# A linear-attention layer and an MLP on one core: a new order of work, w spread by TensorE, and other places for loads and transposes

## The chip, the cores and the metric

The kernel runs on one core of a Trainium2 chip. The core has TensorE (PE, with its weight loads as PEld), VectorE (DVE), ScalarE (ACT), GpSimd (POOL) and SyncE (SP), which here only issues DMAs. The time is the device time of one execution in microseconds; before the change the median of 5 runs is 155.71 us (155.5 to 156.21).

## The reference

There are 4 batches, 8 heads, 768 time steps and 48 elements per head. For each head a state of 48 by 48 is carried through time; then every row of 384 elements is normalized and goes through an MLP of width 1,536 with ReLU, and is added to itself.

```python
for t in range(S):
    kt, vt, rt = (k[:, :, t].copy(), v[:, :, t].copy(), r[:, :, t].copy())
    cur = np.einsum('bhd,bhe->bhde', u[None] * kt, vt)
    y[:, :, t] = np.einsum('bhd,bhde->bhe', rt, state + cur)
    state = w[None, :, :, None] * state + np.einsum('bhd,bhe->bhde', kt, vt)
...
mu = np.mean(x, axis=-1, keepdims=True)
var = np.mean((x - mu) ** 2, axis=-1, keepdims=True)
xn = (x - mu) / np.sqrt(var + 1e-06) * g_ln
ch = np.maximum(xn @ w_ch1, 0.0) @ w_ch2
return (x + ch).astype(np.float32)
```

## The kernel before

The 768 steps of each batch are cut into 6 chunks of 128, which makes 24 tiles of 128 rows. A tile's K, R and V are loaded by SP as 128 partitions by 8 heads of 48 (steps LK, LR, LV, lines 347, 350, 353): 1,024 pieces of 192 bytes each, into rings of 10 buffers.

The decay is put into factors: `Fr` is w to the power of the position and `Fk` w to the power of minus the position less one, both made once by ACT from ln(w) (FR, FK, lines 310 and 307). SR and SK multiply R and K by them. TR transposes both on PE into the PSUM tile `tr`, TC copies them out, AT makes the 128x128 scores of each head, and AM (DVE, line 413) keeps the causal half and writes bf16. S adds up the chunk's keys times values into the state, ZU and ZD scale the state by w to the power of 128; for the tiles in `ZPE` the old state is added on PE by a product with the identity (line 441) and no ZD is needed. Y sums the state's part and the scores' part. The term with u is a number `cc` for each row and head: either PE makes it from the product Q and u's columns (line 434, copied by CC), or, for the tiles in `CC_BY_DVE`, it comes from two products KU and KR and a sum on DVE (line 456). VB (POOL) is that number times V, and X (DVE) adds Y and VB and gives the row's sum.

XN subtracts the mean and gives bf16, SQ (ACT) sums squares, RS (POOL) makes the inverse deviation. The normalized rows are transposed, either by PE and a copy (LT, XT) or by a DMA transpose (LTD). `K_BY_DMA` lists the tiles whose K is transposed by DMA too (TKD, and TRD for R). `GROUPS` says how many tiles go through the first matmul of the MLP together, one or two. UP is one PSUM bank of that matmul (12 instructions of 128 columns for a single tile, 6 of 256 for a pair); its number is 16 times the group, plus which bank. RL is the ReLU. DN is a third of the second matmul of one tile: its number is 4 times the tile, plus the third. OT scales and adds the row, STO stores it.

w1 comes in three thirds of 1,536/3 columns: LW1 loads one as fp32 from SP (line 330), and three steps SW scale it by minus g_ln into bf16 (ACT, DVE or POOL); SW 0 to 2 belong to third 0, 3 to 5 to third 1, 6 to 8 to third 2. For a single tile bank m of UP needs third m. IW2 loads a third of w2 and turns it into bf16 on the way, issued by POOL (line 344). DN third d needs third d of w2 and bank d of the hidden rows.

WU and DU are dummy matmuls on a zero tile that keep PE busy in the head (the number is how many).

All the order is written by hand. `PLAN` is a list of steps "name,number,engine" (v is DVE, s ACT, g POOL); each is emitted in turn, and every engine takes its own instructions in that order, SP its loads, transposes and stores as well. Nothing is reordered later; waits between engines are put in by the framework.

```python
for step in PLAN.split():
    name, i, e = step.split(",")
    steps[name](int(i), e)
```

How w is taken is set by `W_ROWS`. With it WF (line 220) loads w into all 128 partitions, LN (line 268) takes the logarithm of all, and FR and FK read it from SBUF. Without it the row is one partition, and WBM (line 272) spreads its logarithm by an fp32 product with a column of ones into the PSUM tile `y`, which FR and FK read:

```python
RB = P if W_ROWS else 1
...
nc.tensor.matmul(out=t[:, :C], lhsT=ones[:], rhs=ln_b[:], start=True, stop=True)
...
return ln_b[:].rearrange("p (h d) -> p h d", h=H) if W_ROWS else psum["ln"]
```

u's row and g_ln's row are loaded by ACT's queue (RI) after LN; UR on POOL multiplies u by w, and CU on PE turns the rows into columns. The rows of u times w in all partitions, for KU, are made later by UWR from loads LUB (u) and, without `W_ROWS`, LWB (w, line 384).

Of the kernel before, what the change touches and what calls it, by code (L numbers as in the profile page):

```python
# [10 lines left out]
ACT = mybir.ActivationFunctionType  # L11
ENG = mybir.EngineType

GROUPS = [1, 1, 1, 1, 1, 1, 2, 2, 2, 2, 2, 2, 2, 2, 1, 1]
ZPE = [1, 2, 3]
K_BY_DMA = [16, 17, 18, 19, 20, 21, 22, 23]
CC_BY_DVE = [10, 11, 12, 13, 14, 15, 16, 17, 18, 19, 20, 21, 22, 23]
W_ROWS = True
SLOTS = {'kf': 10, 'rf': 10, 'vf': 10, 'sck': 3, 'scr': 3, 'vv': 4, 'trs': 3, 'q': 2, 'A': 2, 'cc': 4, 'ku': 2, 'kr': 2, 'Z': 3, 'ZS': 2, 'Vb': 3, 'x': 13, 'xn': 3, 'xT': 4, 'hT': 4, 'ot': 3}
PLAN = """  # L20
MW,0,v WF,0,- TL,0,s MI,0,g MP,0,v WU,13,- MM,0,g LK,0,- LN,0,s LR,0,- RI,0,s DU,10,-
CL,0,- FR,0,s LW1,2,- FK,0,s SR,0,v SK,0,v DU,12,- TR,0,- WL,0,s LR,1,- LV,0,- UR,0,g
LK,1,- TCk,0,s DU,18,- CU,0,- SR,1,g CV,0,s TCr,0,v LK,2,- SK,1,v AT,0,- LR,2,- UW,0,s
Q,0,v UGC,0,s TR,1,- SW,6,s SW,8,v LV,1,- SW,7,v S,0,- AMa,0,v CC,0,s LV,2,- TCk,1,s
SK,2,g AMb,0,v TCr,1,s LW1,0,- DU,16,- Y,0,- CV,1,s ZU,0,v CV,2,s SR,2,g DU,6,- AT,1,-
Q,1,v VB,0,g DU,5,- TR,2,- AMa,1,v S,1,- TC,2,s AMb,1,v IW2,0,g LW1,1,- IW2,1,g X,0,v
CC,1,s SW,1,s Q,2,v DU,13,- AT,2,- IW2,2,g XN,0,v Y,1,- SW,0,s AM,2,v SW,2,g LT,0,-
SQ,0,s LR,3,- XT,0,v VB,1,g ZU,1,v DU,15,- UP,2,- X,1,v S,2,- RL,2,s SW,3,v SW,5,v
XN,1,s DU,1,- UP,0,- CC,2,v SR,3,v SW,4,s VB,2,g LT,1,- LK,3,- DU,1,- Y,2,- RL,0,s
UP,1,- XT,1,s RS,0,g LV,3,- ZU,2,v UP,18,- SK,3,v SQ,1,s LR,4,- DN,0,- RL,1,s X,2,v  # L30
TR,3,- RS,1,g LK,4,- RL,18,s UP,16,- TC,3,v XN,2,s CV,3,v AT,3,- RL,16,s Q,3,v UP,17,-
SR,4,v SQ,2,s SK,4,g AM,3,v LT,2,- S,3,- RS,2,g LK,5,- XT,2,v Y,3,- TR,4,- CC,3,v
RL,17,s LV,4,- UP,32,- VB,3,g TC,4,s DN,1,- LR,5,- X,3,v RL,32,s UP,34,- Q,4,v XN,3,s
LK,6,- SK,5,v AT,4,- ZU,3,v RL,34,s LT,3,- UP,33,- AM,4,v XT,3,s SQ,3,s CV,4,g UP,50,-
RL,33,s SR,5,v RS,3,g S,4,- RL,50,s Y,4,- CC,4,v TR,5,- ZU,4,v LR,6,- VB,4,g UP,48,-
TC,5,s SK,6,v DN,2,- ZD,4,g LV,6,- X,4,v AT,5,- OT,0,v LV,5,- UP,49,- SQ,4,s Q,5,v
XN,4,s DN,4,- SR,6,v RS,4,g LK,7,- RL,49,s LT,4,- S,5,- DN,5,- XT,4,s CC,5,v LUB,0,-
CV,6,g AM,5,v TR,6,- CV,5,g LR,7,- DN,6,- RL,48,s VB,5,g LK,8,- Y,5,- SK,7,v TC,6,s
UP,64,- UWR,0,g X,5,v LV,12,- UP,66,- XN,5,s Q,6,v SR,7,g AT,6,- RL,64,s LV,7,- OT,1,v
LT,5,- SQ,5,s S,6,- DN,8,- XT,5,v SK,8,g LR,9,- CC,6,v AM,6,v RL,66,s TR,7,- RS,5,g  # L40
UP,81,- LR,8,- ZU,6,v UP,80,- VB,6,g TC,7,v LR,10,- DN,9,- RL,81,s SR,9,g Q,7,v LK,9,-
AT,7,- CV,7,s Y,6,- SR,8,g DN,10,- RL,80,s X,6,v LV,8,- UP,82,- OT,2,v SQ,6,s LK,10,-
S,7,- AM,7,v XN,6,s SR,10,g DN,12,- CC,7,s RL,82,s LR,12,- LT,6,- DN,13,- VB,7,g ZU,7,v
CV,8,s XT,6,v Y,7,- STO,0,- ZD,7,g TR,8,- LK,11,- X,7,v DN,14,- SK,10,g TC,8,v XN,7,s
UP,65,- LV,10,- Q,8,v SK,9,g LT,7,- AT,8,- RL,65,s LK,12,- XT,7,v S,8,- KU,10,v SQ,7,s
UP,96,- SK,11,g OT,3,v LV,9,- CC,8,s TR,9,- AM,8,v UP,101,- VB,8,g TC,9,s LR,11,- DN,16,-
ZU,8,v RS,6,g RL,96,s STO,1,- Y,8,- Q,9,v CV,9,s DN,17,- ZD,8,g LK,16,- X,8,v CV,12,s
S,9,- RL,101,s KR,10,v AT,9,- LK,14,- CC,9,s XN,8,s SK,12,v TR,10,- VB,9,g SQ,8,s AM,9,v
UP,99,- LR,20,- TC,10,s DN,18,- SR,11,g ZU,9,v LV,11,- UP,97,- CV,10,s CC,10,v ZD,9,g RL,99,s
AT,10,- OT,4,v STO,2,- RL,97,s S,10,- KU,12,v LT,8,- LK,13,- DN,20,- XT,8,s ZU,10,v SR,12,g  # L50
CV,11,s Y,9,- AM,10,v STO,3,- DN,21,- VB,10,g LV,13,- TR,11,- X,9,v ZD,10,g DN,22,- TC,11,s
LR,13,- KU,11,v Y,10,- SK,13,g UP,100,- OT,5,v SQ,9,s LK,15,- KR,11,v AT,11,- XN,9,s DN,24,-
LR,15,- SK,14,v RL,100,s KU,13,g X,10,v LT,9,- UP,98,- LR,16,- XT,9,s SR,13,v CV,13,s S,12,-
TR,12,- CC,11,v RL,98,s LV,14,- UP,114,- AM,11,v RS,7,g TC,12,s UP,117,- LK,21,- VB,11,g ZU,12,v
SQ,10,s Y,11,- KR,13,v TR,13,- LR,14,- XN,10,g X,11,v RL,114,s AT,12,- KR,12,v S,13,- RL,117,s
STO,5,- SK,15,v UP,112,- TC,13,s AM,12,v STO,4,- UP,113,- LK,19,- XN,11,s DN,25,- SK,16,g KU,14,v
RL,112,s LR,22,- LT,10,- DN,26,- XT,10,s SR,16,v UP,115,- LK,22,- SQ,11,s SR,14,v OT,6,v Y,12,-
RL,113,s TR,14,- RS,8,g LK,18,- CC,12,v RL,115,s DN,28,- TC,14,s AT,13,- LK,17,- KU,15,v SR,15,v
DN,29,- VB,12,g ZU,13,v LR,17,- TR,15,- AM,13,v UP,116,- ZD,13,g TC,15,s LV,15,- DN,30,- X,12,v
CV,14,g RL,116,s AT,14,- LR,23,- CC,13,v SQ,12,s Y,13,- OT,7,v LT,11,- STO,6,- S,14,- XN,12,g  # L60
DN,32,- XT,11,s KR,14,v LV,18,- VB,13,g LT,12,- KU,16,v UP,132,- TKD,16,- SK,17,g UP,131,- X,13,v
RL,132,s AM,14,v DN,33,- CV,15,s SR,17,g RL,131,s LV,16,- UP,130,- XN,13,s KR,15,v DN,34,- ZU,14,v
XT,12,s LR,18,- RL,130,s KU,17,v Y,14,- ZD,14,g OT,8,v S,15,- LR,19,- AT,15,- CV,18,v SQ,13,s
DN,36,- SK,18,g ZU,15,v STO,7,- UP,129,- CC,14,v LV,20,- ZD,15,g LT,13,- DN,37,- RL,129,v XT,13,s
LV,23,- UP,128,- KR,16,v SR,18,g AM,15,v DN,38,- TRD,16,- RL,128,s UP,133,- CV,16,s VB,14,g OT,9,v
S,16,- TRD,17,- KU,18,v UP,144,- RL,133,s RS,9,g ZU,16,v DN,40,- X,14,v SK,19,g LV,17,- CC,16,v
DN,41,- SQ,14,s UP,145,- SR,19,v LV,19,- DN,42,- CC,15,v VB,16,g RL,144,v XN,14,s LK,20,- Y,15,-
AT,16,- KR,18,v RL,145,s VB,15,g OT,10,v UP,147,- STO,8,- CV,19,s AM,16,v KR,17,g DN,44,- STO,9,-
UP,149,- CV,17,g X,15,v TKD,17,- ZD,16,g DN,45,- RL,147,v Y,16,- RL,149,v KU,19,g UP,148,- X,16,v
CV,20,s STO,10,- LT,14,- XN,15,s CC,18,v SR,20,g DN,46,- XT,14,v SQ,15,s LV,22,- RL,148,v AT,17,-  # L70
# [613 lines left out]
```

## Time and profile before

| | before |
|---|---|
| median of 5 runs | 155.71 us |
| profiled execution | 156.44 us |
| its span, first to last instruction | 154.3 us |
| PE busy, instructions | 143.9 us, 1,788 |
| PEld busy | 117.2 us |
| DVE busy | 110.3 us, 225 |
| ACT busy | 89.5 us, 186 |
| POOL busy | 96.4 us, 133 |
| mean granted TensorE clock | 0.976 |
| DMA moved | 25.98 MB, 168 GB/s |
| packets under 512 B | 87,442 of 92,456 |

The page also gives the busy tenths in 40 slices of 3.86 us, from the start to the end:

```profile
PE   7697995499999999999999999999999999999992
...
DVE  2219962578989789999999699998878876235112
ACT  3537684149777658969966755276454147543440
POOL 3055943051899999998288698999889976100100
PEclk9999999559999999999999999999999999999999
DMA  4998999999989998979999959665454575212211
```

A 9 is 90% or more. The first 10 slices are the head, in which w, the first chunks, w1 and w2 are loaded; the last three are the tail. The page's table of DMA issues gives sizes and the median time from issue to landing:

```profile
kf<-in_k_dram SPq DMA_DIRECT2D x24, 192.0 KB, 4.0
rf<-in_r_dram SPq DMA_DIRECT2D x24, 192.0 KB, 4.5
vf<-in_v_dram SPq DMA_DIRECT2D x24, 192.0 KB, 3.9
...
w_f<-in_moe_w_ch_dram SPq DMA_DIRECT2D x3, 768.0 KB, 6.3
w_sb<-in_moe_w_ch_dram POOLq DMA_DIRECT2D x3, 384.0 KB, 8.9
w_b<-in_w_dram SPq DMA_DIRECT2D x1, 192.0 KB, 3.8
```

Here `w_f` is w1 as it is loaded and `w_sb` both w1 in bf16 and w2. Busy times of PE overlap a little, since its matmuls are pipelined; a row that shows 0.33 us for one matmul may take 0.16 us of PE when others follow.

### The profile page before, as it was taken

To read this page: it belongs to the slowest core of one execution; us is meant where nothing else is said; L and a number is where in the kernel's file an instruction comes from. 1 tells how busy PE (TensorE), PEld (TensorE's weight loads), DVE (VectorE), ACT (ScalarE), POOL (GpSimd) and SP (SyncE) were. 2 spreads that over 40 slices of the span, in tenths; PEclk is the share of its full clock that TensorE was granted. 3 is DMA by queue.
4 is the path that set the end of the run, shared out by engine and by line. 5 is a ranking of instruction groups with operands and counts; after the bars stand their busy time and mean duration, and the time that the engine had idled before them with its cause. 6 is when DMAs were issued, how large, how long until landed. Compare 5 with 4: busy or idle time off the path is not lost.

```text
span 154.3 us, 4487 instructions
## 1 busy us (share of the span) xinstructions
PE 143.9 (93%) x1788; PEld 117.2 (76%) x1788; DVE 110.3 (72%) x225; ACT 89.5 (58%) x186; POOL 96.4 (63%) x133
## 2 busy tenths in 40 slices
PE   7697995499999999999999999999999999999992
PEld 6695883498888688779877787777887777887881
DVE  2219962578989789999999699998878876235112
ACT  3537684149777658969966755276454147543440
POOL 3055943051899999998288698999889976100100
PEclk9999999559999999999999999999999999999999
DMA  4998999999989998979999959665454575212211
GB/s 73 276 232 150 366 240 204 182 197 209 217 174 216 197 226 187 221 153 249 217 197 218 237 105 235 146 102 124 89 148 102 131 164 137 77 55 84 94 55 51
DMA packets 92456, 25.98 MB, mean 168 GB/s; under 512 B 87442, under 2 KB 90900, under 8 KB 92436
## 3 DMA queue, kind: packets, MB, share of 16 engines
q1 hardware_dynamic: 92000, 24.52, 72.8%
q0 software_dynamic: 432, 1.18, 3.9%
q8 instruction: 14, 0.23, 0.7%
q14 instruction: 6, 0.05, 0.1%
q10 hardware_dynamic: 4, 0.00, 0.0%
HBM read 19.27 MB, written 4.72 MB: 155 GB/s over the span
## 4 chain that ended last, share of the span: by engine, by line
PE 79%; SPq 9%; DMA 9%; DVE 1%; issue 1%
PE hp L552 30%; PE o L580 29%; DMA kf<-in_k_dram 9%; PE at L403 5%; PE tr L369 4%; SPq L330 3%; PE y L489 3%; SPq L347 2%; PE s L448 2%; PE y L481 2%; PE tr L537 2%; SPq L353 2%; SPq L350 2%; PE o L595 1%; PE hp L595 1%
## 5 line engine op out<-in xcount | busy, mean ns | idle before, releaser
L552 PE MATMUL hp<-xT,w_sb 128*128 128x128 bf16 (+1 forms) x576 | 58.3, 250 | 0.2 <-DVE xT L206 0.2
L580 PE MATMUL o<-w_sb,hT 128*128 128x384 bf16 x276 | 55.0, 326 | 0.0
L552 PEld LDWEIGHTS <-w_sb 128*128 128x128 bf16 x576 | 49.2, 116 | 4.0 <-issue 0.5
L568 ACT ACTIVATE hT<-hp 128x512 bf16<-128x512 f32 x65 | 38.0, 597 | 23.2 <-PE hp L552 22.6
L580 PEld LDWEIGHTS <-hT 128*128 128x128 bf16 x276 | 24.8, 98 | 11.1 <-issue 0.2
L413 DVE TENSOR_TENSOR A<-at,mask 128x1024 bf16<-128x1024 f32 (+1 forms) x26 | 29.3, 1133 | 1.0 <-PE at L403 0.7
L636 DVE SCALAR_TENSOR_TENSOR ot<-o,rs,x 128x384 f32<-128x384 f32 x23 | 14.1, 613 | 16.7 <-PE o L580 15.0
L471 POOL TENSOR_TENSOR Vb<-vf,cc 128x384 f32<-128x384 f32 x24 | 20.9, 875 | 5.1 <-DVE cc L206 3.1
L209 POOL TENSOR_TENSOR sck<-kf,Fk 128x384 bf16<-128x384 f32 x15 | 15.9, 1064 | 11.1 <-DMA kf<-in_k_dram 7.5
L503 ACT ACTIVATE sqj<-x,sm 128x384 bf16<-128x384 f32 x24 | 14.8, 615 | 10.1 <-DVE x L496 10.1
L204 ACT COPY trs<-tr 128x1024 bf16<-128x1024 bf16 (+1 forms) x14 | 12.8, 924 | 7.0 <-PE tr L369 7.0
L517 POOL TENSOR_SCALAR rs<-sq 128x1 f32<-128x1 f32 (+1 forms) x16 | 3.8, 235 | 19.6 <-ACT sqj L503 18.8
L496 DVE SCALAR_TENSOR_TENSOR x<-y,Vb 128x384 f32<-128x384 f32 x24 | 13.2, 549 | 3.5 <-PE y L489 2.6
L209 POOL TENSOR_TENSOR scr<-rf,Fr 128x384 bf16<-128x384 f32 x14 | 14.6, 1045 | 1.1 <-DMA rf<-in_r_dram 1.0
L509 ACT ACTIVATE xn<-x,sm 128x384 bf16<-128x384 f32 x17 | 10.4, 614 | 6.3 <-DVE x L496 6.3
L209 POOL TENSOR_TENSOR Z<-ZS,WLZ 128x384 bf16<-128x384 f32 x13 | 13.5, 1037 | 0.8 <-DVE ZS L465 0.8
L209 DVE TENSOR_TENSOR scr<-rf,Fr 128x384 bf16<-128x384 f32 x10 | 6.5, 656 | 8.4 <-DMA rf<-in_r_dram 4.2
L262 PE MATMUL o<-warm 128*128 128x128 bf16 x110 | 10.6, 264 | 1.0 <-DVE warm L227 1.0
L520 POOL TENSOR_TENSOR rs<-rs,expo 128x1 f32<-128x1 f32 (+1 forms) x16 | 10.0, 623 | 1.3
L204 ACT CAST vv<-vf 128x384 bf16<-128x384 f32 x14 | 7.1, 513 | 6.4 <-PE y L489 3.5
L489 PE MATMUL y<-vv,A 128*128 128x48 bf16 x192 | 8.9, 184 | 1.1 <-DVE A L413 1.1
L403 PE MATMUL at<-trs 48*128 48x128 bf16 x192 | 9.7, 222 | 0.0
(81 smaller groups left out, 189.1 us busy)
## 6 DMA issues: line engine op xcount, KB each, us to landing
kf<-in_k_dram SPq DMA_DIRECT2D x24, 192.0 KB, 4.0
rf<-in_r_dram SPq DMA_DIRECT2D x24, 192.0 KB, 4.5
vf<-in_v_dram SPq DMA_DIRECT2D x24, 192.0 KB, 3.9
out_dram<-ot SPq DMA_DIRECT2D x23, 192.0 KB, 3.0
w_f<-in_moe_w_ch_dram SPq DMA_DIRECT2D x3, 768.0 KB, 6.3
w_sb<-in_moe_w_ch_dram POOLq DMA_DIRECT2D x3, 384.0 KB, 8.9
w_b<-in_w_dram SPq DMA_DIRECT2D x1, 192.0 KB, 3.8
u_b<-in_u_dram SPq DMA_DIRECT2D x1, 192.0 KB, 3.8
```

Of the source, the lines that this page charges most:

```text
L204: nc.scalar.copy(out=out, in_=in_)
L209: engines[e].tensor_tensor(out=out, in0=in0, in1=in1, op=ALU.mult)
L403: nc.tensor.matmul(out=t[:, par, q, :], lhsT=trs(i)[p0 : p0 + D, 1, q, :], rhs=trs(i)[p0 : p0 + D, 0, q, :], start=True, stop=True,)
L413: nc.vector.tensor_tensor(out=AA(i)[:, a:b].rearrange("p e q t -> p (e q) t"), in0=psum["at", i][:, a:b].rearrange("p e q t -> p (e q) t") ...
L471: nc.gpsimd.tensor_tensor(out=Vb(i)[:].rearrange("p (h d) -> p h d", h=H), in0=vf(i)[:], in1=cc(i)[:].unsqueeze(2).to_broadcast([P, H, D]) ...
L489: nc.tensor.matmul(out=t[:, h * D : (h + 1) * D], lhsT=AA(i)[:, par, q, :], rhs=vv(i)[:, h, :], start=first, stop=True, skip_group_check=True,
L496: nc.vector.scalar_tensor_tensor(out=xx(i)[:], in0=psum["y", i][:, :C], scalar=1.0, in1=Vb(i)[:], op0=ALU.mult, op1=ALU.add, accum_out=sm[ ...
L503: nc.scalar.activation(out=sqj[:], in_=xx(i)[:], func=ACT.Square, bias=sm[i][:], scale=-float(C), accum_out=sq[g][:, j : j + 1])
L552: nc.tensor.matmul(out=t[:, a * gw : (a + 1) * gw], lhsT=w1_sb[n][kc][:, fb::FB], rhs=xT(g)[:, kc, :gw], start=(kc == 0), stop=(kc == CK - 1),
L568: nc.scalar.activation(out=o, in_=s, func=ACT.Relu)
L580: nc.tensor.matmul(out=psum["o", i][:, :C], lhsT=hT(g)[:, fk, j * P : (j + 1) * P], rhs=w2_sb[d][:, a, :], start=(fk == 0), stop=(fk == FK ...
L636: nc.vector.scalar_tensor_tensor(out=ot(i)[:], in0=psum["o", i][:, :C], scalar=rs[g][:, j : j + 1], in1=xx(i)[:], op0=ALU.mult, op1=ALU.add,)
```

## The change

Only the constants and the plan change.

- `W_ROWS` is off: one row of w is loaded, WBM spreads its logarithm, and LWB loads w into all partitions later (before UWR).
- SP's order in the head: K and R of tile 0, V1, K2, R1, K1, V0, R2, K3, V2, then third 1 of w1, R3, third 0, V3, K4, third 2, R4 and the other chunks. Before it was K0, R0, third 2, R1, V0, K1, K2, R2, V1, V2, thirds 0 and 1, R3, K3, V3, R4, K4.
- w2's three loads stand elsewhere in POOL's order: two after XN of tile 0, one after SR3 and SW5. Before all three followed VB of tile 0. SW5, SW0, SW7, SW8 and SW6 are on POOL now; before only SW2 was.
- UP of the first tiles goes 1, 0, 16, 33, 32, 17, 34, 2; before it went 2, 0, 1, 18, 16, 17, 32.
- Rows of tiles 12 to 15 are transposed by DMA (LTD) as well as those of 16 to 23; R of tile 16 goes back to PE.
- Groups: 7 pairs instead of 8, and the last four tiles single. Tile 9's `cc` goes to DVE, tile 3 leaves `ZPE`.
- Fewer dummies in the head: 66 instead of 110.
- The rest of the order is new all through, with steps on other engines.

```diff
-GROUPS = [1, 1, 1, 1, 1, 1, 2, 2, 2, 2, 2, 2, 2, 2, 1, 1]
-ZPE = [1, 2, 3]
+GROUPS = [1, 1, 1, 1, 1, 1, 2, 2, 2, 2, 2, 2, 2, 1, 1, 1, 1]
+ZPE = [1, 2]
 K_BY_DMA = [16, 17, 18, 19, 20, 21, 22, 23]
-CC_BY_DVE = [10, 11, 12, 13, 14, 15, 16, 17, 18, 19, 20, 21, 22, 23]
-W_ROWS = True
+CC_BY_DVE = [9, 10, 11, 12, 13, 14, 15, 16, 17, 18, 19, 20, 21, 22, 23]
+W_ROWS = False
-MW,0,v WF,0,- TL,0,s MI,0,g MP,0,v WU,13,- MM,0,g LK,0,- LN,0,s LR,0,- RI,0,s DU,10,-
-CL,0,- FR,0,s LW1,2,- FK,0,s SR,0,v SK,0,v DU,12,- TR,0,- WL,0,s LR,1,- LV,0,- UR,0,g
-LK,1,- TCk,0,s DU,18,- CU,0,- SR,1,g CV,0,s TCr,0,v LK,2,- SK,1,v AT,0,- LR,2,- UW,0,s
-Q,0,v UGC,0,s TR,1,- SW,6,s SW,8,v LV,1,- SW,7,v S,0,- AMa,0,v CC,0,s LV,2,- TCk,1,s
-SK,2,g AMb,0,v TCr,1,s LW1,0,- DU,16,- Y,0,- CV,1,s ZU,0,v CV,2,s SR,2,g DU,6,- AT,1,-
-Q,1,v VB,0,g DU,5,- TR,2,- AMa,1,v S,1,- TC,2,s AMb,1,v IW2,0,g LW1,1,- IW2,1,g X,0,v
-CC,1,s SW,1,s Q,2,v DU,13,- AT,2,- IW2,2,g XN,0,v Y,1,- SW,0,s AM,2,v SW,2,g LT,0,-
-SQ,0,s LR,3,- XT,0,v VB,1,g ZU,1,v DU,15,- UP,2,- X,1,v S,2,- RL,2,s SW,3,v SW,5,v
-XN,1,s DU,1,- UP,0,- CC,2,v SR,3,v SW,4,s VB,2,g LT,1,- LK,3,- DU,1,- Y,2,- RL,0,s
-UP,1,- XT,1,s RS,0,g LV,3,- ZU,2,v UP,18,- SK,3,v SQ,1,s LR,4,- DN,0,- RL,1,s X,2,v
-TR,3,- RS,1,g LK,4,- RL,18,s UP,16,- TC,3,v XN,2,s CV,3,v AT,3,- RL,16,s Q,3,v UP,17,-
-SR,4,v SQ,2,s SK,4,g AM,3,v LT,2,- S,3,- RS,2,g LK,5,- XT,2,v Y,3,- TR,4,- CC,3,v
+MW,0,v WF,0,- TL,0,s MI,0,g WU,13,- MP,0,v LN,0,s MM,0,g LK,0,- WBM,0,- RI,0,s LR,0,-
+FR,0,s LV,1,- DU,4,- CL,0,- FK,0,s SR,0,v LK,2,- SK,0,v WL,0,s DU,3,- TR,0,- LR,1,-
+UR,0,g TCk,0,v LK,1,- SK,2,g DU,2,- CU,0,- TCr,0,s SR,1,v LV,0,- Q,0,v AT,0,- UGC,0,s
+LR,2,- SK,1,v AMb,0,v DU,3,- TR,1,- CV,0,s LK,3,- UW,0,s AMa,0,v S,0,- SR,2,v LV,2,-
+Y,0,- TC,1,v CC,0,s LW1,1,- DU,9,- AT,1,- ZU,0,v VB,0,g Q,1,v CV,1,g X,0,v DU,9,-
+TR,2,- CV,2,g S,1,- XN,0,g TC,2,s AM,1,v LR,3,- IW2,0,g SW,3,s LW1,0,- CC,1,v IW2,1,g
+Q,2,v DU,13,- Y,1,- SW,4,s ZU,1,v LT,0,- VB,1,g SK,3,v SQ,0,s DU,1,- S,2,- SR,3,g
+DU,1,- AT,2,- X,1,v XT,0,s AM,2,v XN,1,s SW,5,g DU,6,- TR,3,- CC,2,s SQ,1,s IW2,2,g
+TC,3,v DU,1,- UP,1,- SW,2,v SW,1,s SW,0,g AT,3,- ZU,2,v LT,1,- RL,1,s Y,2,- AM,3,v
+LV,3,- VB,2,g UP,0,- XT,1,s RS,0,g LK,4,- RL,0,s X,2,v DU,1,- UP,16,- CV,3,s XN,2,g
+DN,0,- LW1,2,- RS,1,g SQ,2,s Q,3,v Y,3,- LT,2,- RL,16,s S,3,- SK,4,v XT,2,s CC,3,v
+UP,33,- ZU,3,v VB,3,g UP,32,- RL,33,s SW,7,g X,3,v UP,17,- SW,8,g RL,32,v XN,3,s LR,4,-
+RL,17,s SW,6,g LT,3,- LK,5,- DN,1,- XT,3,v RS,2,g UP,34,- SR,4,v LR,5,- SQ,3,s UP,2,-
+RL,34,s RS,3,g SK,5,v LV,4,- TR,4,- RL,2,s UP,50,- SR,5,g TC,4,s UP,49,- RL,50,s AT,4,-
...
+KU,16,g CV,17,s LTD,12,- X,13,v AT,14,- RL,130,s DN,38,- XN,13,v ZD,14,g SQ,13,s AM,14,v UP,131,-
+TKD,16,- TR,16,- RS,9,g RL,131,s S,15,- OT,9,v AT,15,- LTD,13,- KR,16,g Y,14,- ZU,15,v DN,40,-
+AM,15,v TCr,16,s ZD,15,g S,16,- DN,41,- LK,20,- CV,18,s X,14,v SK,17,g AT,16,- STO,9,- ZU,16,v
+UP,145,- XN,14,s LK,22,- CC,16,v UP,144,- SQ,14,s SK,18,v VB,16,g DN,42,- RL,145,s TRD,17,- KU,17,v
+RL,144,s Y,15,- KU,18,g UP,149,- OT,10,v TKD,17,- KR,17,v DN,44,- CV,19,g RL,149,s X,15,v DN,45,-
+SR,19,g CC,17,v SQ,15,s TRD,18,- AM,16,v UP,146,- XN,15,g UP,148,- RS,10,g LTD,14,- SK,19,v RL,146,s
...
```

## The prediction

> **What bounds the kernel now.** I read the busy time by stage first.
>
> ```profile
> 10.00:20.00 10.00, 8.67 (x158) 7.49 (x158) 8.43 (x17) 6.69 (x15) 7.06 (x9) 1.00 0.98 254
> 20.00:25.00 5.00, 4.92 (x78) 4.08 (x77) 1.76 (x6) 4.34 (x11) 2.34 (x5) 1.00 1.13 217
> 25.00:30.00 5.00, 1.39 (x14) 1.22 (x15) 2.40 (x6) 0.56 (x2) 0.00 (x0) 0.73 1.00 196
> 30.00:35.00 5.00, 5.00 (x66) 4.44 (x64) 3.78 (x7) 1.94 (x6) 2.57 (x5) 0.58 1.00 193
> ...
> 60.00:80.00 20.00, 20.00 (x265) 16.07 (x262) 19.70 (x39) 17.07 (x36) 15.79 (x19) 1.00 0.94 202
> 80.00:100.00 20.00, 19.99 (x221) 16.02 (x219) 18.03 (x39) 11.07 (x24) 16.90 (x21) 1.00 0.94 192
> ```
>
> The columns are PE, PEld, DVE, ACT, POOL, granted clock, DMA share, GB/s. From 29 us to 140 us PE has no pause: that part is bound by PE's own work. The 25:30 row is the hole: PE works 1.39 of 5 us, POOL nothing, while the DMA engines are full (1.00). The 30:35 row is its echo, a clock of 0.58 at full PE. The clock's records have half rate from 27.33 to 34.15 us. The chain that ended last names what opened the hole, PE's timeline its length:
>
> ```profile
> 15.23 13.14 DMA kf<-in_k_dram
> 28.37 0.02 issue
> 28.39 0.57 DVE sck L209
> 28.96 0.04 issue
> 29.01 0.61 PE tr L369 x4
> 29.62 1.28 PE hp L552 x12
> ```
>
> ```profile
> 24.16 0.81 PE L580 MATMUL o<-w_sb,hT 128*128 128x384 bf16 x4
> 26.60 0.40 PE L369 MATMUL tr<-ident,scr 128*128 128x128 bf16 x4 [1.63 <-DVE scr L209]
> 29.01 0.61 PE L369 MATMUL tr<-ident,sck 128*128 128x128 bf16 x4 [2.01 <-DVE sck L209]
> ```
>
> K of tile 3 needed 13.14 us to land where the median is 4.0. Two issue lists say why:
>
> ```profile
> 12.02 2.64 SPq L330 DMA_DIRECT2D w_f<-in_moe_w_ch_dram  x2
> ...
> 15.23 1.45 SPq L347 DMA_DIRECT2D kf<-in_k_dram  x1
> 16.73 4.82 SPq L353 DMA_DIRECT2D vf<-in_v_dram  x1
> ```
>
> ```profile
> 16.37 1.85 POOL L344 DMA_DIRECT2D w_sb<-in_moe_w_ch_dram  x3
> ```
>
> In the trace's DMA packets w2 runs from 20.29 to 27.7 us. Before and after that the 16 engines pass about 1,100 chunk packets (192 B) per us, so a chunk load of 1,024 takes 0.95 us; during it they pass 70. A w2 packet takes about 0.22 us on its engine against 0.015, and they alternate. So the head lost 3.64 us of pause and half of the 5.2 us from 29.0 to 34.2: 6.2 us.
>
> **The change, part by part.**
>
> *w as one row.* The 128 packets of w_b (1.75 to 4.04 us) become one. Before, ln starts 0.46 us after the last (4.50). Now about 2.5: first packet 1.75, as before, and about 0.75 for packet and semaphore. ln takes 0.52, to 3.0. Then the fp32 product of ones and ln (L272, new). The nearest row is the 128x384 bf16 matmul of L441, 0.16 us of PE at full clock and 0.32 at half. The Trainium skill ("FP8 and Floating Point Precision", TensorE Precision Notes) says that true fp32 goes through the array in four passes: an estimate of 0.64 or 1.28 us. L281 shows two records per fp32 instruction, so 0.32 by the row alone. I take 1.28, since PE is cold then (0.115 us per dummy). The factors are ready at 5.6 instead of 6.50 us. This sets no end; chunk loads start about 0.8 us sooner, which does count.
>
> *Four chunks before w1.* By 0.95 us per load from 2.7 us, ten loads (K 0 to 3, R and V 0 to 2) leave the queue at 12.2. w1 behind them: first packet 2.8 us after issue and 2.2 us for a third (before: 14.79 to 17.57, 17.57 to 19.74). Third 1: 12.8 to 15.2, landed 15.9. R3: 16.1, landed 16.9. Third 0: 18.3, landed 18.9. V3 would be 18.3 to 19.2.
>
> *w2.* GpSimd's queue now is UR 0.98, SK2 1.0, VB0 1.0, two CV of 0.50, XN0 0.59, and then two of the three issues. u_row comes about 1.4 us sooner (ln ends 3.0 instead of 5.0, some queueing kept), UR ends at 8.1, the columns at 9.5, scores of tile 0 at 10.1, its two masks (0.6 each) at 11.35. DVE then does SR2, TC1, ZU0, Q1 and X0 (0.5, 0.7, 0.5, 0.35, 0.55), to 14.1. XN0 ends at 14.75: issues at 14.75 and 15.5. First packets came 3.92 us after the first issue (16.37 to 20.29); so 18.7. The third issue stands behind VB1, SR3 (R3 landed 16.9) and SW5 (0.75): about 18.9. w2 then flows from 18.7 for 6.7 us, to 25.4. The Trainium skill ("DMA: Bandwidth & Descriptors", SWDGE vs HWDGE vs iDMA, and the table of latencies) gives about 1 us to GpSimd's first byte. By it w2 starts at 15.8 and catches R3: SR3, SW5, the first up-projection and the third issue slip from 18.9 to 22.7 us, but w2 is through by 26.5 and the last third of w1 lands at 28.7; that sum ends near 153.5. The row decides: 3.92.
>
> *Where the stall goes.* V3 is caught instead of K3: 0.4 us of its packets before 18.7, 460 more in 6.7 us, the rest after, landed 26.5. Behind it: CV3 on ACT, with SQ2, RL16 and XT2 behind; Y3 on PE, with everything. Up to there PE does UP 1, 0 and 16 and DN0 (19 to 22.7; UP1 waits for SW5, DN0 for w2). A pause of about 4.3 us, and again half clock. After Y3 (27.0) come Y3, LT2, S3, UP33, UP32, UP17, LT3, DN1: 0.36+0.17+0.27+3x0.67+0.17+0.65 = 3.6 us, twice that at half clock: 34.2; 32.7 if the clock returns at 30.75 (its windows are 3.41 us: 27.33, 30.75, 34.15). Middle 33.4. Next is UP34, which needs third 2 of w1: K4 until 27.1, third 2 until 29.3, landed 30.0, then SW7, SW8, SW6, all three on POOL at 0.75 behind VB3: 32.5. It just fits.
>
> Before, PE has at 34.15 done six UP (2, 0, 1, 18, 16, 17), DN0 and tiles 0 to 3 without LT3. After, at 33.4, six UP, DN0, DN1 and LT3 too: 0.82 us more. Head: 34.15-33.4+0.82 = 1.6 us gained. Not all of 6.2: the bytes are the same and the DMA engines are full until about 30 us in both.
>
> *Dummies.* 110 become 66; at 0.056 us warm they are fillers, priced at zero as long as PE waits anyway. The Trainium skill ("TensorE: Matmul & The Clock Gate", Part 1) wants about one busy window of 3.4 us for full clock, which speaks against the cut. The row: before, 61% busy from 3.4 to 6.85 did not raise the clock, 70% from 13.7 to 17.1 kept it. By my sum 75 to 100% of 6.9 to 17 us stays busy at the cold rate, so UP1 starts warm.
>
> *The body.* Rows by DMA for tiles 12 to 15: four LT of 0.17 off PE (-0.68), four XT off ACT and DVE. TR16's r half returns (+0.22), tile 3's identity product goes (-0.16), tile 9's four small products go (-0.11), two tiles in groups of one instead of a pair (+0.045 each). PE: -0.64. Each added transpose costs SP 1.19 us of issue and lands in 2.3 (before's eight); LTD12 and LTD13 wait on SP for xn, with TKD16 and loads of tiles 20 and up behind them, whose rings of 10 are tiles ahead. PE has about 3.5 us between LTD13 and its use: hidden, up to 1 us if the queue is late. TRD16 leaves SP, the load of w_b for all rows (0.7) comes.
> KU, KR and the sum of tile 9 (0.36+0.45+0.45), UWR and more SK and TC go to DVE; counting every step at its mean, DVE rises by 3.4 us, POOL by 5.5 (five w1 scalings instead of one, ZD3), ACT falls by 4.7. Between 24 and 40 us of PE work DVE has 16.3 us against 16.1 of PE, where it had 13.9: the cover is gone there. I take +0.7 (0 to 2).
>
> Sum: -1.6-0.64+0.7 = -1.5 us. The profiled execution took 156.44 (span 154.3, 2.1 around it): 154.9 for it. The median 155.71 is 0.73 lower; I put the sum there: 154.2.
>
> **The rivals.**
> *The stall goes away (chance 0.13).* V3 lands before w2's packets, which needs them only 0.7 us later. Y3 flows, and third 2 of w1 is the only wait. Against: K4 and w1 are then caught, UP34 still waits until about 32. Head at best 3.4 us: 152.4.
> *A second cold stretch (0.25, slower).* Place: UP34. Third 2 lands last, and POOL alone scales it (2.2 us) behind VB3, which hangs on S3 and CC3. If SW6 ends more than some 2 us after DN1, PE falls below the busy share that held the clock (43% lost it, 70% kept it) and is halved once more, for 3.4 to 6.8 us of work: 1.7 to 3.4 lost, plus the wait of 2, less the 2.2 gained elsewhere: 157.3. For it: my fit at 32.5 has no slack.
> *DVE becomes the bound (0.14).* The full 2 us of the 24 to 40 stretch: 155.6, no change to speak of.
> *Cold from the start (0.08).* The clock stays half through the first UPs: 2 to 3 us: 156.9.
>
> **How the numbers follow.** Likeliest (0.40): 154.2, its own range 152.9 to 155.2. Faster 0.53 (0.40+0.13), within 0.3% (0.47 us, about what can be told) 0.12, slower 0.35 (0.25+0.08 and 0.02 of DVE). Low end: the second case less 1.2 for its error, 151.2; high end: the cold stretch plus 0.7, 158.0.
>
> **What would show it.** Right: ln at about 2.5 us; w2's first packets near 18.7; V3 the longest landing; a pause of PE before Y3 with half clock after; UP34 near 33. Wrong: R3 caught, another pause at UP34, PE with gaps between 50 and 80 us, or no half clock at all after 20 us.

## The result, and the profile after

The changed kernel takes 154.40 us (median of 44 runs, 152.78 to 157.93); the kernel before, run beside it, 155.87 us (79 runs). The ratio is 0.9916, with a 95% interval of 0.9896 to 0.9936: about 1.3 us faster. The forecast was 154.2 us and -1.5 us. Times here and below are medians of all executions, ratios compare only those within 1.5% of their kernel's fastest, and since the first profiled execution of the changed kernel was its slowest of all (157.93 us), the lines below come from a second one (155.12 us, span 153.2; the first experiment).

In that experiment's file the plan is packed into fewer lines: its line numbers are 10 lower than the changed kernel's (L542 is UP, L527 LT, L359 TR, L570 DN). Other experiments are shifted by a few lines too; the names tell which step it is.

Busy time by stage of the changed kernel (PE, PEld, DVE, ACT, POOL, granted clock, DMA share, GB/s):

```profile
10.00:20.00 10.00, 8.88 (x151) 7.78 (x149) 9.17 (x18) 5.75 (x16) 7.36 (x11) 1.00 1.06 274
20.00:25.00 5.00, 4.58 (x85) 3.94 (x80) 2.95 (x6) 3.52 (x8) 3.40 (x7) 1.00 1.11 232
25.00:30.00 5.00, 2.19 (x32) 1.88 (x30) 2.27 (x6) 1.75 (x4) 2.03 (x3) 0.94 0.90 236
30.00:35.00 5.00, 5.00 (x60) 4.33 (x58) 1.64 (x3) 2.65 (x6) 4.61 (x8) 0.71 1.07 211
40.00:60.00 20.00, 19.13 (x271) 14.95 (x270) 20.00 (x38) 13.11 (x26) 15.18 (x20) 1.00 0.86 188
```

The same view of the kernel before, the stretch that the prediction did not show:

```profile
40.00:60.00 20.00, 20.00 (x297) 16.12 (x295) 17.55 (x35) 13.79 (x29) 18.78 (x24) 1.00 1.01 207
```

The hole is still at 25 to 30 us (2.19 us of PE where there were 1.39), its echo is half as deep (clock 0.71 instead of 0.58: one window of 3.41 us at half rate, 29.45 to 32.86, instead of two). New is the 40:60 row: DVE is busy 20.00 of 20 us, PE only 19.13, where before PE had all 20 and DVE 17.55.

What opens the hole is read in two views. The chain of work followed back from the stretch of 18 to 34 us of the changed kernel (start, duration, what):

```profile
13.64 13.00 DMA kf<-in_k_dram
26.64 0.02 issue
26.66 0.56 DVE sck L199
27.22 0.09 DVE cc L196
27.31 0.07 issue
27.38 0.84 POOL Vb L461
28.22 0.02 issue
28.24 0.58 DVE x L486 x2
28.82 0.02 issue
28.84 0.62 ACT xn L499
29.47 0.05 issue
29.51 0.50 PE tr L527 x3
```

PE's timeline and, last, POOL's, of the same execution:

```profile
18.32 0.40 PE L359 MATMUL tr<-ident,scr 128*128 128x128 bf16 x4 [0.84 <-POOL scr L199]
...
29.51 0.50 PE L527 MATMUL tr<-ident,xn 128*128 128x128 bf16 x3 [2.80 <-ACT xn L499]
...
31.09 2.36 PE L542 MATMUL hp<-xT,w_sb 128*128 128x128 bf16 x24
```

```profile
28.80 2.02 POOL L331 TENSOR_SCALAR w_sb<-w_f,g_neg 128x512 bf16<-128x512 f32 x3 [0.59 <-DMA w_f<-in_moe_w_ch_dram]
```

A load of K again needs 13 us, but it is K4, not K3 (before) and not V3 (forecast). Tile 4 is not wanted yet; but its scaling SK4 stands on DVE ahead of tile 3's CC3, so VB3, X3, XN3 and LT3 of tile 3 wait for K4: 2.80 us of PE. The last third of w1, caught with it, is scaled by POOL from 28.80, and UP34 follows at 31.09.

All of the span can be put into four terms: the first matmul's start, PE's busy time, PE's pauses, and what lies behind the last matmul.

| us | before | changed |
|---|---|---|
| first matmul | 0.97 | 0.97 |
| PE busy | 143.87 | 143.14 |
| PE pauses to 20 us | 2.69 | 1.16 |
| pauses 20 to 36 us | 3.69 | 3.23 |
| pauses after 36 us | 0.04 | 1.16 |
| after the last matmul | 3.00 | 3.52 |
| span | 154.27 | 153.19 |

So pauses in the head fell by 2.0 us, pauses of the body rose by 1.1, PE's busy time fell by 0.73 and the tail grew by 0.5. The busy time holds the half clock: at half rate the 5.1 us of work from 29.0 to 34.15 us before cost about 2.6 us, in the changed execution the 3.35 us from 29.51 to 32.86 about 1.7. It also holds a longer cold start: the clock is full from 12.38 us on, before from 10.26.

A part of the gain lies outside the span. An execution takes longer than its span by 1.85 us on average in the 44 of the changed kernel, and by 2.08 in each set of executions of the kernel before, with a spread of 0.05 within a kernel. So 0.2 of the 1.3 us is not in the table; what it is, no trace shows.

### The profile page after: what moved, and what is told of

Read it like the earlier page. It is cut to its first block, busy times and chain, and to the rows that moved or that the text cites. A ratio compares the mean times of both kernels' runs of the same rounds, so it can differ in the third digit from the quotient of the medians.

```text
span 156.1 us, 4453 instructions
## 1 busy us (share of the span) xinstructions
PE 144.9 (93%) x1769; PEld 117.0 (75%) x1769; DVE 115.1 (74%) x228; ACT 84.9 (54%) x172; POOL 102.8 (66%) x143
## 4 chain that ended last, share of the span: by engine, by line
PE 61%; DVE 12%; DMA 11%; SPq 10%; issue 2%; POOL 2%; DVEq 0%
PE hp L552 26%; PE o L580 22%; DMA w_f<-in_moe_w_ch_dram 8%; SPq L347 3%; DMA out_dram<-ot 3%; PE at L403 3%; DVE A L413 3%; PE tr L369 3%; SPq L330 3%; SPq L353 2%; SPq L350 2%; DVE ot L636 2%; POOL w_sb L341 2%; DVE scr L209 2%; PE y L489 2%
## 5 line engine op out<-in xcount | busy, mean ns | idle before, releaser
L552 PEld LDWEIGHTS <-w_sb 128*128 128x128 bf16 x612 | 50.8, 116 | 6.0 <-POOL w_sb L341 1.6
L568 ACT ACTIVATE hT<-hp 128x512 bf16<-128x512 f32 x56 | 33.0, 593 | 37.3 <-PE hp L552 37.1
L204 ACT COPY trs<-tr 128x1024 bf16<-128x1024 bf16 (+1 forms) x15 | 14.2, 950 | 5.9 <-PE tr L369 4.7
L209 POOL TENSOR_TENSOR sck<-kf,Fk 128x384 bf16<-128x384 f32 x12 | 12.4, 1036 | 3.0 <-DMA kf<-in_k_dram 1.9
L209 POOL TENSOR_TENSOR scr<-rf,Fr 128x384 bf16<-128x384 f32 x12 | 12.7, 1063 | 2.1 <-DMA trs<-scr 1.1
L509 ACT ACTIVATE xn<-x,sm 128x384 bf16<-128x384 f32 x15 | 9.2, 614 | 8.7 <-DVE x L496 8.7
L570 DVE TENSOR_SCALAR hT<-hp 128x512 bf16<-128x512 f32 x16 | 10.9, 684 | 2.8 <-PE hp L552 2.5
L209 DVE TENSOR_TENSOR scr<-rf,Fr 128x384 bf16<-128x384 f32 x12 | 8.7, 724 | 4.0 <-DMA rf<-in_r_dram 4.0
L209 DVE TENSOR_TENSOR q<-trs 128x512 bf16<-128x512 bf16 x9 | 5.2, 580 | 5.7 <-ACT trs L204 5.7
L209 DVE TENSOR_TENSOR sck<-kf,Fk 128x384 bf16<-128x384 f32 x12 | 6.7, 556 | 3.3 <-DMA kf<-in_k_dram 2.9
```

Source lines behind the costliest of these rows:

```text
L204: nc.scalar.copy(out=out, in_=in_)
L209: engines[e].tensor_tensor(out=out, in0=in0, in1=in1, op=ALU.mult)
L552: nc.tensor.matmul(out=t[:, a * gw : (a + 1) * gw], lhsT=w1_sb[n][kc][:, fb::FB], rhs=xT(g)[:, kc, :gw], start=(kc == 0), stop=(kc == CK - 1),
L568: nc.scalar.activation(out=o, in_=s, func=ACT.Relu)
L570: nc.vector.tensor_relu(out=o, in_=s)
```

## The experiments

Each is compared with the kernel before on the same chip; ratios are to that. The experiments were run on three chips, and the changed kernel was repeated on one only, beside the fillers and the chunks. Where the others are set against its 0.9916 or 0.9926, that assumes that the ratio holds from chip to chip, which was not tried. Progress is told by the second matmul (DN): the start of the instruction that follows the first n of its 288 (before, n = 48 at 59.07 us, n = 128 at 94.40; changed 56.34 and 93.00).

### The changed kernel again

No edit.

> The changed kernel unaltered, for a second trace. In its first trace w2's packets began at 18.9 us, V3 had landed before them, and K of tile 4 and third 2 of w1 were caught instead; PE paused 2.0 us before the transpose of tile 3's rows and 1.25 us before UP34, and ran at half clock from 31.3 to 38.1 us. Theory (a load caught by w2, whichever is next in SP's queue): the same two pauses again, in the same places within 1 us. Rival (the clock alone): places and lengths of the pauses as before, but the half clock comes or goes with its free-running windows and the time follows it by up to 3.4 us.

Measured: 154.97 us, ratio 0.9926 (0.9884 to 0.9968). The result stands, and this is the trace read above.

### Fillers in the pauses

If half clock is what the pauses cost, dummies in them should give it back. Into the changed kernel (DF is DU with another target in PSUM):

```diff
+DU,20,-  (before TR,3)
+DF,30,-  (before LT,3)
+DF,20,-  (before UP,34)
```

> The changed kernel with dummies in PE's three pauses: 20 before TR3, 30 before the transpose of tile 3's rows, 20 before UP34 (into unused columns of a PSUM bank; the result is the same). If the half clock after the pauses costs what its records say (6.8 us at half rate, of which about 5.5 under work), it goes and the kernel is 1 to 2.5 us faster than the changed one on the mean. If the pauses alone cost, and the clock does not matter since loads are late anyway, the time stays within 0.4 us of the changed kernel's.

Into the kernel before:

```diff
+DF,62,-  (before TR,3)
```

> The kernel before with 62 dummies between DN0 and TR3, which fill the pause of 3.6 us from 25.0 to 28.6 us. By the theory that half of the head's loss was the clock, it is 1.5 to 2.6 us faster than the kernel before, and as fast as the changed kernel or faster. If the late K3 alone cost, under 0.4 us.

Measured: 158.26 us, ratio 1.0087 (1.0043 to 1.0131), and 158.97 us, ratio 1.016 (1.0112 to 1.0208). Both slower, which neither the theory nor its rival had. The traces show that the fillers did their first duty: no half clock from 14.5 us on. The changed kernel with fillers is only 0.3 us ahead until n = 160 (105.48 against 105.79) and 0.6 behind at n = 240 (137.01 against 136.39). The kernel before with its filler is 1.7 us ahead at n = 48 and n = 128 (57.37, 92.71); at n = 144 it is level (101.79 against 101.93). The waits of that kernel, 88 to 97 us (us in total, times, longest):

```profile
ACT vv L194 <- DMA vf<-in_v_dram: 3.2, 1, 3.2
DVE scr L199 <- DMA trs<-scr: 1.8, 1, 1.8
...
PE hp L549 <- DVE hT L567: 1.3, 1, 1.3
```

PE waits 1.25 us at 94.2 for DVE, which was held by a transpose by DMA (its buffer of scaled R was still being read), and ACT by a load: the lead ran into SP's queue. The transpose of tile 16's K (TKD16) stands there in SP's timeline, before and with the filler:

```profile
80.25 1.55 SPq L528 DMA_TRANSPOSE trs<-sck  x1
```

```profile
83.07 1.29 SPq L525 DMA_TRANSPOSE trs<-sck  x1
```

So while PE is 1.7 us earlier, this queue is 2.8 us later; from 57 to 97 us most of it runs 1.6 to 3.1 us late, and why is not shown. Before, the DMA engines are busy nearly all of the time from 40 to 100 us (DMA share 1.01, 0.94, 0.94), and PE waits for 0.04 us in all after 36 us. The two medians lie 2.1 and 1.6 us above the executions that were traced (156.19 and 157.36 us); that part stays open.

### The loads of late tiles moved back in SP's queue

That queue carries loads of tiles 20 to 23 as early as 56 us. Moved behind the work of tiles 16 to 19, without and with the filler:

```diff
-LR,20 LV,20 LK,21 LR,22 LK,22 LR,23 LV,23   (56 to 86 us)
+LR,20 LV,20 after LV,19; LK,21 after LK,20; LR,22 LK,22 LR,23 LV,23 after STO,10
```

> The kernel before with only SP's order changed from 55 us on: seven loads of tiles 20 to 23 (R20, V20, K21, R22, K22, R23, V23), which stood at 56 to 85 us ahead of what tiles 16 to 19 need, stand behind the loads of tile 19 and 20. Theory (SP's queue is full from 33 to 99 us and is as late as PE at 90 us, so a head gained is given back there): PE still has the 3.6 us of pause and the half clock in the head, so alone this is worth 0 to 0.7 us; the time should now follow the clock. Rival (the late queue was the bound all along): faster by 1.5 us or more.

> The same, and 62 dummies in PE's pause of the head, as in the kernel that filled the pause alone (which was 1.6% slower than before). Theory (two bounds side by side): now the 1.7 us that the fill gains in the head last to the end, 1.2 to 2 us faster than before. Rival (dummies there do harm by themselves, by something that their trace does not show): slower than before again, by 2 us or more.

Measured: 157.85 us, ratio 1.015 (1.0081 to 1.0219); with the filler 157.91, ratio 1.0164 (1.0089 to 1.0239). The move let TKD16 go 1.4 us and TRD16 2.6 us sooner (78.87 and 83.66), but then seven loads stood ahead of the next transposes: TKD18 slipped from 97.65 to 102.50 us, TRD18 from 100.31 to 105.04. Waits of the kernel without filler, 100 to 125 us:

```profile
POOL scr L199 <- DMA trs<-scr: 2.6, 1, 2.6
DVE kr L199 <- POOL scr L199: 2.3, 1, 2.3
...
PE at L393 <- DMA trs<-scr: 0.8, 1, 0.8
```

It is level with the kernel before until n = 144 and 2.3 us behind at n = 240. Without the filler neither expectation came: the order of the queue was no slack that could be shifted in this way. In this trace the transposes of tiles 16 to 19 run against PE, and the move only changes which of them are late. With the filler the time is the rival's, but as the moved loads cost 1.5% without any filler, it does not tell whether fillers do harm of their own.

### The first chunks ahead of all of w1

The kernel before with eleven chunk loads ahead of w1 (SW6, SW8, SW7 moved to just before UP2, behind their load):

```diff
-LW1,2 LW1,0 LW1,1 among the chunks
+... LV,2 LR,3 LK,3 LW1,2 LW1,0 LW1,1
```

> The kernel before with one part of the change: K, R of tile 3 and the other first chunks ahead of all of w1 (w1's thirds in the same order 2, 0, 1, their third-2 scalings moved to just before UP2). By the theory the stall moves to V3 or the next load that w2 catches: faster by 0.3 to 1.5 us. If the order of the loads was the whole gain, faster by 1.3 us or more; if it was none of it, within 0.3 us or slower.

Measured: 160.25 us, ratio 1.0182 (1.0116 to 1.0247). PE's timeline:

```profile
29.51 1.47 PE L542 MATMUL hp<-xT,w_sb 128*128 128x128 bf16 x12 [11.83 <-ACT w_sb L327]
```

With w2 in the same place of POOL's order (its packets run from 15.05 to 26.7 us), w2 catches w1 itself (14.48 to 28.6), and PE stands 11.8 us before its first up-projection. Two thirds of w1 are through at 25.6 us; in the changed kernel they are at 18.1, just after w2 starts (17.74).

But this is no clean test of the chunks' place, for the edit added a wait of its own. ACT's timeline:

```profile
26.90 1.34 ACT L327 ACTIVATE w_sb<-w_f,g_neg 128x512 bf16<-128x512 f32 x2 [11.18 <-DMA w_f<-in_moe_w_ch_dram]
28.74 0.71 ACT L327 ACTIVATE w_sb<-w_f,g_neg 128x512 bf16<-128x512 f32 x1
```

The last row is SW6, which UP2 waits for. Its third of w1 landed at 23.61 us, but SW6 now stands on ACT behind SW1 and SW0 (the first row), whose third landed only at 26.82. By an estimate from these rows UP2 could have started some 5 us sooner. What the chunks' place is worth alone stays open.

### w by rows again

The changed kernel without WBM and LWB:

```diff
-W_ROWS = False
+W_ROWS = True
-WBM,0,-   LWB,0,-
```

> The changed kernel with one part undone: w loaded into all 128 partitions at the start, no product with ones, no second load of w. The first chunks should land about 0.7 us later and the factors be ready about 1 us later; by the step that let the later loads count, 0.3 to 0.8 us slower than the changed kernel; if the head is bound by w2 and w1 alone, within 0.3 us.

Measured: 155.52 us, ratio 1.0003 (0.9973 to 1.0034): against the changed kernel's ratios from the other chips, this part is worth 0.8 to 0.9%, 1.3 us, more than either expectation. The traced execution was the longest of 20 (157.79 us). With the rows, ln starts at 4.40 us instead of 2.02, and the first four chunk loads are through at 7.10 instead of 6.31 us. From there 0.8 us goes through loads and transposes to the last third of w1. PE's timeline:

```profile
32.28 1.70 PE L542 MATMUL hp<-xT,w_sb 128*128 128x128 bf16 x24 [2.13 <-POOL w_sb L331]
```

UP34 starts 1.2 us later than in the changed kernel, after a wait of 2.13 us, and a window of half clock follows (33.50 to 36.91). Such a window is not the rule: 11 of the 20 executions have a mean clock of 0.994 or more and took 154.9 us on average, the other nine 156.3.

### Rows of tiles 12 to 15 by PE again

```diff
-LTD,12 LTD,13 LTD,14 LTD,15
+LT and XT (ACT) of tiles 12 to 15
```

> The changed kernel with one part undone: rows of tiles 12 to 15 by PE and a copy on ACT instead of by DMA. By the sum that adds PE's work it is 0.7 us slower than the changed kernel (four transposes of 0.17 us); if what lies behind them on SP mattered more than PE, it is as fast or faster.

Measured: 155.09 us, ratio 1.0005 (0.9978 to 1.0031), against 0.9916 and 0.9926 on other chips: about 1.3 us lost. Its traced execution kept full clock, as did that of the reordered head below (SK4 later), which has the rows by DMA; between those two PE's busy time is 142.5 against 141.8 us: 0.7 us for the four transposes, as the prediction's 0.68. Another 0.4 us lies outside the span: its 20 executions take 2.27 us more than their spans, those of the changed kernel 1.85. The trace shows 0.57 us of pause at 88 us (TR16 waits for the copy XT13) but the same span, 152.4 us, with a shorter tail.

### Rings of four for scaled K and R

```diff
-'sck': 3, 'scr': 3
+'sck': 4, 'scr': 4
```

> The changed kernel with rings of four instead of three buffers for the scaled K and scaled R. Theory (after 90 us the scaled R waits for its buffer, which a late transpose by DMA still reads): the matmuls of the second product from the 160th on are 0.5 to 1 us sooner and the ratio is 0.985 to 0.989. Rival (the buffer is free in time where TensorE does not wait; the small gaps come from VectorE's order): unchanged, 0.990 to 0.994.

Measured: 154.77 us, ratio 0.9948 (0.9902 to 0.9994), no better than the changed kernel and outside of both expected ranges. From n = 48 to n = 240 it takes 80.65 us, the changed kernel 80.05. The buffers are free in time where PE sets the pace.

### K4's scaling behind tile 3

The chain above names one step. It is moved:

```diff
-S,3 SK,4,v XT,2 CC,3,v
+S,3 XT,2 CC,3,v ... XT,3,v SK,4,v
```

> The changed kernel with one step moved: the scaling of tile 4's K on VectorE goes behind the copy of tile 3's transposed rows (before, it stood ahead of tile 3's correction and held VectorE 2.9 us for K4). Theory (K4, caught by w2, reaches tile 3 only through this place in VectorE's order; behind it stands the last third of w1, which lands at 29.7 us and needs 2.7 us of GpSimd): the pause of TensorE before the transposes of tile 3's rows falls from 2.8 us to under 1, and the same time appears before up-projection 34, which still starts at 31 to 32.5 us. Time against the kernel before 0.988 to 0.996, as the changed kernel's 0.992. Rival (tile 3 alone sets the head): up-projection 34 starts 2 us sooner and the ratio is about 0.98.

Measured: 154.73 us, ratio 0.9914 (0.9865 to 0.9962). PE's timeline:

```profile
25.96 2.35 PE L542 MATMUL hp<-xT,w_sb 128*128 128x128 bf16 x36 [0.30 <-ACT xT L194]
28.15 0.33 PE L527 MATMUL tr<-ident,xn 128*128 128x128 bf16 x3
28.31 0.81 PE L570 MATMUL o<-w_sb,hT 128*128 128x384 bf16 x4
31.30 1.53 PE L542 MATMUL hp<-xT,w_sb 128*128 128x128 bf16 x24 [2.17 <-POOL w_sb L331]
```

No pause before LT3 (28.15) is left, and UP34 starts at 31.30 (31.09 before the move), after 2.17 us of waiting: the theory to the letter. The two waits lie one behind the other; taking the first away gives its time to the second.

### Both waits of the head taken away

In addition the last third of w1 is scaled by three engines, and work that doesn't need it is put ahead of UP34:

```diff
-SW,7,g SW,8,g SW,6,g ... UP,34
+SW,6,g ... SW,8,v SW,7,s UP,49 UP,48 UP,34
```

> The same, and the last third of w1 scaled by VectorE, ScalarE and GpSimd together instead of by GpSimd three times, and the up-projections 49 and 48 of tile 3 (which need no last third) ahead of 34. Theory of the head (both waits behind w2 are hidden now): no pause of TensorE over 1.2 us after 20 us, no half clock between 20 and 40 us, the 48th matmul of the second product 1.5 to 2.5 us sooner than in the changed kernel (56.3), ratio 0.978 to 0.984. Theory of the later bound (what the head gains, VectorE at 20.0 of 20 us between 40 and 60 us and the transposes by DMA take back, as they did with the dummies in the pauses): sooner at the 48th, level again by the 160th to 240th, ratio 0.99 to 1.0.

Measured: 154.31 us, ratio 0.9919 (0.9874 to 0.9964). The head does what was meant: full clock from 14 us to 92 us, pauses of 20 to 36 us down from 3.23 to 2.11 us, n = 48 at 54.42, 1.9 us sooner than in the changed kernel. In the traced execution (156.70 us, the second longest of 12) it is lost at one place. By stage, then waits (78 to 94 us), then the chain followed back from 96 us:

```profile
80.00:100.00 20.00, 18.13 (x193) 14.00 (x191) 15.71 (x29) 12.09 (x25) 17.17 (x21) 0.91 0.79 147
```

```profile
PE hp L542 <- DMA xT<-xn: 1.9, 1, 1.9
```

```profile
86.34 0.98 POOL Z L199
87.32 0.02 issue
87.34 0.12 DVE ZS L455
87.46 4.17 DMA xT<-xn
91.64 0.04 issue
91.68 1.91 PE hp L542 x12
```

The up-projection of tiles 12 and 13 waits 1.9 us for LTD13. SP issues LTD13 at 87.46 us, 88.29 in the changed kernel: PE is 1.9 us earlier, SP's queue 0.8. That uses up what LTD13 had in hand, and the pause itself is its landing, which took 4.17 us here and 2.34 in the changed kernel (the least of the two in its view of `xT`, 82 to 96 us):

```profile
DMA to landing us min/median/max: 2.3/3.0/3.6
```

What made it late is not shown. A window of half clock follows (92.55 to 95.97), and n = 144 comes at 101.01, later than the changed kernel's 99.41. Eight of the 12 executions had no such window; they took 153.83 us on average (their spans 151.7), the four at full clock of the kernel with only SK4 moved 153.94 (152.1), which in its trace is 1.3 us later at n = 48. So most of the lead is lost there too, and where was not traced.

### And the rows of tiles 12 and 13 by PE

```diff
-LTD,12 LTD,13
+LT,12 XT,12,s LT,13 XT,13,s
```

> The changed kernel with the new order of the head (K4's scaling behind tile 3's rows, last third of w1 scaled by three engines, up-projections 49 and 48 ahead of 34), and the rows of tiles 12 and 13 transposed by TensorE again instead of by DMA. Theory (the head's gain of 1.9 us was lost at one place, 89.8 us, where the up-projections of tiles 12 and 13 waited 1.9 us for the transpose of tile 13's rows, which SP issues behind loads, stores and another transpose, 1.2 us each): that pause is gone, the 128th matmul of the second product starts at 91.0 to 91.8 instead of 93.4 (changed kernel 93.0), the 240th at 134 to 135, ratio 0.978 to 0.986. Rival (SP's row of ten transposes after 91 us, which is where it was, takes the lead back at the next place): a pause of 1 to 2 us between 96 and 125 us, the 240th at 136 or later, ratio 0.99 to 0.995.

Measured: 155.07 us, ratio 0.9894 (0.9849 to 0.9938), not to be told from the changed kernel's 0.9916, and between the two expected ranges. The pause at 89.8 us is gone, but n = 128 comes at 92.53, not at 91.0 to 91.8. PE's waits, 84 to 94 us:

```profile
PE tr L359 <- ACT xT L194: 0.6, 1, 0.6
```

Of the 1.5 us of lead at n = 112, 1.07 are gone by n = 128: 0.34 for the two transposes, 0.57 for TR16, which waits for the copy XT13, the rest in small pieces. Neither theory had it: no pause of SP's making over 0.42 us appears later, and in this trace the lead is spent on PE itself.

## Why the prediction was right, and where it was not

**The sum.** Forecast -1.5 us; measured -1.3 us. Its three terms do not come out one by one. The head's -1.6 us was too small: the traces have 2.0 us of pauses less and 0.9 us less lost at half clock. The four transposes of PE's -0.64 us were found as 0.7 us of busy time. DVE's +0.7 us was found as 1.1 us of new pauses after 36 us, 0.87 of them in the 40:60 row where DVE has 20.00 of 20. That makes -2.5 us, while the two traced spans differ by 1.1. The other 1.4 us were priced at nothing: 0.5 us of tail, and about 0.9 us of busy time, most likely in the head, where full clock comes 2.1 us later. So the sum is in part luck: too small a gain, and costs of about the same size that were left out.

The DVE term was right in kind. Gaps of PE had been named as a sign of being wrong ("PE with gaps between 50 and 80 us"); those of 0.45, 0.21 and 0.15 us at 45.9, 55.6 and 56.2 us fit the cover that the third term had priced.

**w's row.** ln starts at 2.02 us (forecast 2.5). WBM takes 1.64 us in two records, at half clock; forecast 1.28 by the four passes that the Trainium skill ("FP8 and Floating Point Precision", TensorE Precision Notes) gives to fp32, against 0.32 by the row of L281. The rule was near and the row far off. The factors are ready at 5.39 us (5.6).

**w2's start: a step that failed, with no harm to the sum.** "First packets came 3.92 us after the first issue; so 18.7": POOL reached the issue at 14.90 us as forecast (14.75), but the packets began at 17.74, 2.84 us after. In the nine profiled executions with the new head this took from 1.95 to 2.96 us. The 3.92 is not chance either: three variants of the kernel before have 3.81 to 3.96. It belongs to that head, where two thirds of w1 run without a break around the issue (14.5 to 21.3 us in the one with the filler); in the variant with the chunks first, whose w1 starts only after the issue, it is 1.98. What else is in the queues may explain it, but nothing here varied that alone. The Trainium skill's figure of about 1 us ("DMA: Bandwidth & Descriptors", the table of latencies) was not met either.

**"V3 is caught instead of K3": wrong.** V3, issued at 13.11 us, was in before 18.80. What w2 caught were K4 (13.0 us to landing) and the last third of w1. That was the rival "the stall goes away", which had K4 and w1 caught and UP34 waiting until 32; it was wrong that the stall then goes: K4 held tile 3 by its place in DVE's order, which the prediction had not looked for ("Behind it: CV3 ..." was asked of V3 only; the question what stands behind SK4 on DVE was not put). The pause came before LT3 instead of Y3, 2.80 instead of 4.3 us, with one window of half clock instead of two. UP34 started at 31.09 (forecast 33.4, its need 32.5). The move of SK4 shows why two wrong steps did the sum little harm: UP34 hangs on the last third, and whatever stalls ahead of it is covered by that wait.

**The second cold stretch at UP34.** Its place was right: without the early row of w the wait there is 2.13 us and half clock follows. Its price is smaller: 1.3 us more than the changed kernel all told, if ratios of two chips may be compared, where the rival stood 3.1 us above the likeliest case. (Its own terms, 1.7 to 3.4 and 2 less 2.2, give 157.2 to 158.9 us, not 157.3 as the middle; those of the DVE rival 155.5, not 155.6.)

**Dummies and warm start.** The first UP ran at full rate, as taken. But full clock came at 12.38 us in this trace and at 12.99 to 16.43 in the eight others with the new head; in the kernel before it came at 10.26, in its variants at 4.24 to 10.16. That the cut from 110 to 66 dummies costs nothing is not shown: no run put them back.

**"From 29 us to 140 us PE has no pause: that part is bound by PE's own work": only half true.** A row without pauses shows who works, not what is in hand behind it. Three experiments brought PE to the body 1.7 to 1.9 us sooner, and lost it near 90 us in their traces: two to SP's transposes and loads, one to PE's own transposes in their place. The kernel before says the same without any edit. Its executions with a mean clock of 0.994 or more took 155.79, 154.62 and 154.76 us on average in the first set on each of the three chips (7, 10 and 7 executions), those with 0.982 or less 156.29, 155.04 and 155.60 (15, 17 and 17). So two and more windows of half clock go with 0.4 to 0.8 us at the end, where the prediction counted 2.6. A gain of the head is worth its size only as far as what stands behind has slack.

**What stays open.** The fillers' medians lie above their traces. Of the 1.3 us that the rows by PE cost, 0.7 us are PE's and 0.4 us lie outside the span, unexplained; what is left, and the worth of w's row, hang on ratios of different chips. Why SP's queue was later with the filler, and what the chunks' place is worth alone, no run shows.

## What to carry to other kernels

When a load is late, look for every step that stands behind its first reader on that reader's engine: a tile that nobody needs yet can hold the tile that everybody needs. A pause that is removed must be followed to the next wait, and a lead to the next queue with a fixed pace; move both or neither. And when one part of a change is tried alone, look at the order on every engine that it touches: ahead of w1 the chunks came with a scaling that now stood behind two others, and the 1.8% that this kernel lost says little of the chunks.

## What the runs showed of the hardware

**The half clock is decided in windows.** The clock's records change only on a grid of 3.41 us. In the 14 profiled executions I took PE's busy share of each window after 13 us and the clock of the next. All windows at full clock with a share up to 0.45 (seven of them, the tail left out: 0, 0.20, 0.25, 0.38, 0.42, 0.43, 0.45) were followed by half clock; all with 0.50 or more (0.50, 0.56, 0.57, 0.58, 0.59, 0.61 and up) kept it. To come back took more: the window of 27.33 to 30.74 us before, busy for 51%, was followed by a second one at half clock, that of 29.45 to 32.86 in the changed kernel, 98%, by full clock. The grid stands differently in each execution, so the same pause can cost or not: UP34's wait of 2.13 us left 38% of its window (half clock), one of 2.17 us 50% of its (none). It shows in times too: over 56 executions of the changed kernel, the 30 with a mean clock of at least 0.992 took 154.0 us on average, the 23 from 0.982 to 0.992 (one window at half) 155.25.

**Products of a single row seem to count for little in it.** Before 13 us the busy share alone does not decide: in the changed kernel PE is busy for 99 and 100% of the windows of 2.14 to 5.55 and 5.55 to 8.97 us, and the clock stays half (a dummy takes 0.115 us there, 0.056 later). Much of that is CL, CU and WBM, products of one row. Left out of the share, they leave 33 and 46%. By that count the 14 executions agree on the way back to full clock: every window at half clock with up to 78% was followed by half clock, every one with 80% or more by full clock. Two windows of the variants of the kernel before that lost full clock though busy for 77 and 90% come to 42 and 55%; the second still stands outside the rule above. No run varied these products alone, so this is a reading of traces and not a test.

**The large packets of w2 hold back the small ones.** While w2 runs in the changed kernel (17.74 to 25.9 us), chunk packets fall from about 1,100 per us to between 49 and 132 in six of the eight microseconds, in most of these about one for each of w2 (from 19 to 20 us 55 against 59); the load that is in the queue then takes 13 us instead of 4. A packet of w2 takes 0.25 us on its engine (the prediction read 0.22), one of a chunk 0.015. The bytes are not lost, but one tile's chunk is late, and the order of the loads says which one.
